# Norm rows in the activation buffer, weight-sum work in eighths, score requests per channel tile

## The chip, the cores and the metric

The kernel runs on one core of one Trainium2 chip. The time is device microseconds of that core for one execution; the comparison number is the median of several. TensorE (PE) multiplies matrices, PEld is its loading of weights, VectorE (DVE) works element by element, ScalarE (ACT) applies functions and copies, GpSimd (POOL) is used only to build constants, SyncE (SP) issues nearly all DMAs. Every engine executes its own instructions in program order and waits on semaphores for the others.

## The reference

Two layers, each a sliding attention block A and a gated feed-forward block B, with residuals; the weights are the same in both layers. x is 2048 tokens by 1024 in bf16.

```python
def _A_ref(x, wqkv, wo):          # 32 heads of 32
    W, dil = 8, 2
    ...                           # q, k, v = x @ wqkv
    idx = pos[:, None] - off[None, :]      # off = 0, 2, ..., 14
    logits = jnp.einsum("bhsd,bhswd->bhsw", q, kg) * scale
    attn = _softmax(logits, axis=-1)       # masked before the start
    o = jnp.einsum("bhsw,bhswd->bhsd", attn, vg)
    return o... @ wo
def _B_ref(x, w1, w3, w2):        # 1024 -> 3584 -> 1024
    return (silu(x @ w1) * (x @ w3)) @ w2
x = A_x
x = x + _A_ref(_layernorm(x, axis=-1), A_wqkv, A_wo)
x = x + _B_ref(_layernorm(x, axis=-1), B_w1, B_w3, B_w2)
x = x + _A_ref(_layernorm(x, axis=-1), A_wqkv, A_wo)
x = x + _B_ref(_layernorm(x, axis=-1), B_w1, B_w3, B_w2)
```

A token attends to itself and to seven earlier ones at steps of two.

## The kernel before, in words

**Units and order.** Tokens are cut into four chunks of 512; a unit is a layer and a chunk, so there are eight units, (layer 0, chunks 0 to 3) and (layer 1, chunks 0 to 3). First comes QKV of layer 0 for all chunks (`first_q` for q of chunk 0, then `q_part` for the rest, L682). Then, for each unit u, `b_stage` (L854) does its feed-forward; in units 1 to 4 it is followed by layer 1's QKV of unit u+3. Attention is worked in halves of 256 tokens, 16 in all, on VectorE, beside the matrix work of TensorE.

**The planner.** The order on each engine is written out by the program itself. It keeps an estimated clock per engine (`now`, moved by `pe`, `dve` and `act` with fixed costs) and queues of small steps for VectorE: norms, sums, value steps, score steps, in this priority. `background(until)` (L130) emits from the queues whatever fits before a given estimated time. The order is therefore fixed when the program is built; an engine that is late in reality still waits in that order.

**Norms.** `norm_stats` (L203) and `norm_apply` (L223) normalise a 128-token tile: statistics L210, L213, L215, then L234 writes the normalised rows `xn` (128 by 1024, fp16) to one of three buffers of the pool `xnp`, and L237 issues a DMA transpose on SP that puts them into `xnT`, the operand of the next matmuls. A buffer is free again when its transpose has landed. The key of a norm is ("Q", layer, chunk) for QKV and ("B", layer, chunk) for the feed-forward. `hT` (L171), 128 by 16 by 512 bf16, holds the feed-forward activations (L895, L792; read at L908); `first_q` keeps q of chunk 0 in its first eight slices (L339, stored by L386).

**Attention on VectorE.** For a half, `score_steps` (L460) multiplies q by shifted k eight times (L475) and folds them in a tree into `psm` (L399, L401); then a gather on TensorE (L488) sums over the head's channels into `L`; softmax L507 to L519 (the exponential on ScalarE, L511); then four spreads on TensorE (L528), each copied by ScalarE into `At` (L530). `value_steps` (L540) multiplies At by shifted v (L559) and folds into `oT`. `o_tile` (L630) multiplies oT by wo (L646) and adds it to x (L651); after a half's second tile the feed-forward norm is queued. The score steps of the next half start when the four spreads are out.

**Requests to TensorE.** A gather or a spread is put into `pe_queue` with its estimated time. `pe_requests(limit=1)` (L454) puts up to `limit` of them into TensorE's order, those whose time plus 1.5 us has come by TensorE's estimated clock. It is called by `between` (L665), which also loads due weights and places output tiles: in QKV after two channel tiles (16 matmuls), in `b_stage` of units 0 and 1 before every block of 128 features, in the w2 products after each accumulator, in `products` (L760, units 2 to 7) after each product. `between(..., must=True)` places all queued output tiles, and forces the value and score steps they need inline; in a unit it stands at L923, at the second accumulator of the last w2 stage's first half, where `hold` is not set.

**Feed-forward.** Units 0 and 1 (u < TU) do it directly. A group is four blocks of 128 features; per block (`fi`) come eight matmuls with w1 (L883), silu to `sg` on ScalarE (L887), eight matmuls with w3 (L891), and L895 on VectorE, hT = sg * up. Groups 0 to 3 are the first split, 4 to 6 the second; each split ends with the w2 products (L908). Units 2 to 7 use a seven-product scheme (`products`) on sums of weight blocks, which units 0 (w1) and 1 (w3) make on the way, in `prepare` (L748):

- `measure` (L715): ScalarE takes the sum of absolute values of the group's weight tile; its output goes to a scratch that covers the first 4096 columns of `big`;
- `scales` (L721): a small matmul (L724) sums over partitions, four small VectorE operations make a power-of-two scale and its inverse;
- `transform(a)` (L734), a = 0, 1: four scaled copies on ScalarE (L739) into block a of `big`, four differences on VectorE (L744), and a DMA to DRAM (`t_d`, L746). Block 0 lies inside the scratch of `measure`, block 1 does not.

One of these four steps stands at the end of each block of the group:

```python
        if fi == 0:
            measure(u, g, w)
        elif fi == 1:
            scales(u, g)
        elif fi == 2:
            transform(u, g, w, 0)
        else:
            transform(u, g, w, 1)
```

Weights come in tiles of 1 MB through six buffers (`wp`), loaded in the order `seq`; a group's two tiles are given back by `release(2)` and reloaded at the next `between`.

Of the kernel before, what the change touches and what calls it, by code (L numbers as in the profile page):

```python
# [17 lines left out]
def kernel(  # L18
# [129 lines left out]
    def bank(name):  # L148
        return psum.tile([P, 512], FP32, name=name, tag="mm")
# [73 lines left out]
    def norm_apply(key, c, r):  # L223

        if key not in xnTs:
            xnTs[key] = xtp.tile([P, KT, CH], FP16, name="xnT")
        xnT = xnTs[key]
        mv, sd, ready = moments[key, r]
        rstd = small.tile([P, 2], FP32, name="rstd")

        def apply(i):
            j = 2 * r + i
            xn = xnp.tile([P, D], FP16, name="xn")
            nc.vector.tensor_scalar(xn[:], x_sb[:, c * TPC + j, :], mv[:, i, 0:1], rstd[:, i:i + 1],  # L234
                                    op0=ALU.subtract, op1=ALU.mult)
            with hp():
                nc.sync.dma_start_transpose(out=xnT[:, :, j * P:(j + 1) * P], in_=xn[:])  # L237
            xnT_at[key] = now["dve"] + DMA
            norm_left[key] = norm_left.get(key, TPC) - 1

        yield 0.10, ready, lambda: nc.vector.reciprocal(rstd[:], sd[:])
        for i in range(2):
            yield 0.47, 0.0, lambda: apply(i)
# [421 lines left out]
    def between(hold, must=False):  # L665

        flush()
        pe_requests()
        while o_queue and (must or oT_at.get((o_queue[0][0], o_queue[0][1] // 2), 1e9) + 0.3 <= now["pe"]):
            o_tile()  # L670
            if not must:
                break
        while norm_queue and not hold:
            queue_norm(*norm_queue.pop(0))
            if not norm_queue and sum_queue:
                adds.append([sum_later(sum_queue.pop(0)), None])
# [5 lines left out]
    def q_part(l, c, which, ws, then=()):  # L682

        ready = ready_norm(("Q", l, c))
        xnT = xnTs[("Q", l, c)]
        first = (l, c, which) == (0, 0, 1)
        if first:
            qT = qkvp.tile([P, KT, TCH], BF16, name="qT")
            kT = qkvp.tile([P, KT, HALO + TCH], BF16, name="kT")
            nc.vector.memset(kT[:, :, 0:HALO], 0.0)  # L690
        for t0 in range(0, KT, SG):
            sgt = stg.tile([P, SG, CH], BF16, name="sgt")
            for t in range(t0, t0 + SG):
                ps = bank("ps")
                for kk in range(KT):
                    nc.tensor.matmul(ps[:], lhsT=ws[kk // KH][:, kk % KH, t::KT], rhs=xnT[:, kk, :],  # L696
                                     start=(kk == 0), stop=(kk == KT - 1))
                r = pe(KT, ready)
                background(r)
                nc.scalar.copy(sgt[:, t - t0, :], ps[:])  # L700
                done = act(0.6, r)
                if first:
                    nc.scalar.copy(kT[:, t, HALO:], ps[:, 0:TCH])
                    done = act(0.4)
            nc.sync.dma_start(qkv_d[l][which][:, t0:t0 + SG, c * CH:(c + 1) * CH], sgt[:])
            if first and t0 == SG:
                load_part(qT, 0, 0, 0, False)
            between(False)
            if t0 // SG < len(then) and then[t0 // SG]:
                then[t0 // SG]()  # L710
        qkv_at[l, c, which] = done + DMA / 2
        if first:
            qks[0, 0] = qT, kT, done + 0.1
# [17 lines left out]
        nc.vector.reciprocal(down, up)  # L731
        dve(0.8, r)

    def transform(m, g, w, a):  # L734

        b = blocks[a]
        KQ = KT // 2
        for i, (kh, fh) in ((0, (0, 0)), (1, (0, 1)), (3, (1, 0)), (5, (1, 1))):
            nc.scalar.activation(b[:, i], w[:, kh * KQ:(kh + 1) * KQ, fh * 256 + a * P:fh * 256 + (a + 1) * P],  # L739
                                 ACTF.Copy, scale=up_scale[:, m, g:g + 1])  # L740
        r = act(2.9, now["dve"] + 0.1)
        background(r)
        for out, x, y in ((4, 5, 1), (1, 1, 0), (2, 5, 1), (6, 3, 2)):
            nc.vector.tensor_tensor(b[:, out], b[:, x], b[:, y], op=ALU.subtract)  # L744
        dve(1.4, r)
        nc.sync.dma_start(t_d[m][g][:, a, :], b.rearrange("p b k c -> p (b k c)"))  # L746

    def prepare(u, g, fi, w1t, w3t):  # L748

        w = (w1t, w3t)[u]  # L750
        if fi == 0:
            measure(u, g, w)
        elif fi == 1:
            scales(u, g)
        elif fi == 2:
            transform(u, g, w, 0)
        else:
            transform(u, g, w, 1)

    def products(u, f0, f1, hold):  # L760

# [92 lines left out]
    def b_stage(u, hold):  # L854
# [7 lines left out]
        for (f0, f1) in fsplits:  # L862
            lastsplit = (f1 == fsplits[-1][1])
            if u >= TU:
                th = products(u, f0, f1, hold)
                if lastsplit:
                    sums_free[0] = True
            for g0 in range(f0, f1, FG) if u < TU else ():
                gn = min(FG, f1 - g0)
                w1t, w3t = weight("w1"), weight("w3")  # L870
                for fi in range(gn):
                    f = g0 + fi
                    slack = 1.0 if f < f1 - 2 else -0.5
                    if f < f1 - 1:
                        between(hold)
                    else:
                        flush()
                    if f == 8 and 1 <= u and u + 3 < len(units):
                        lq, cq = units[u + 3]
                        queue_norm(("Q", lq, cq), cq, range(R))  # L880
                    pg = bank("pg")
                    for kk in range(KT):
                        nc.tensor.matmul(pg[:], lhsT=w1t[:, kk, fi * P:(fi + 1) * P], rhs=xnT[:, kk, :],  # L883
                                         start=(kk == 0), stop=(kk == KT - 1))
                    r = pe(KT, ready)
                    sg = sgp.tile([P, CH], BF16, name="sg")
                    nc.scalar.activation(sg[:], pg[:], ACTF.Silu)  # L887
                    ts = act(0.6, r, "silu")
                    pu = bank("pu")
                    for kk in range(KT):  # L890
                        nc.tensor.matmul(pu[:], lhsT=w3t[:, kk, fi * P:(fi + 1) * P], rhs=xnT[:, kk, :],  # L891
                                         start=(kk == 0), stop=(kk == KT - 1))
                    r = max(pe(KT), ts)
                    background(r + slack)
                    nc.vector.tensor_tensor(hT[:, f - f0, :], sg[:], pu[:], op=ALU.mult)  # L895
                    th = dve(0.64, r)
                    prepare(u, g0 // FG, fi, w1t, w3t)
                release(2)
            for hh in range(2):
                w2ts = [weight("w2") for g0 in range(f0, f1, 8)]  # L900
                for j in range(TPC):
                    n = c * TPC + j
                    final = u == len(units) - 1 and lastsplit and hh == 1 and j == TPC - 1
                    step = 256 if final else 512
                    for q0 in range(0, 512, step):
                        acc = psum.tile([P, step], FP32, name="acc", tag="mm")
                        for f in range(f0, f1):
                            nc.tensor.matmul(acc[:], lhsT=hT[:, f - f0, j * P:(j + 1) * P],  # L908
                                             rhs=w2ts[(f - f0) // 8][:, (f - f0) % 8, q0:q0 + step],
                                             start=(f == f0), stop=(f == f1 - 1))  # L910
                        if q0 == 0:
                            pe(f1 - f0 - 1)
                            r = pe(1, th)
                            background(r + 1.0)
                            dve(0.64, r)
                        o0 = hh * 512 + q0
                        xs = x_sb[:, n, o0:o0 + step]
                        nc.vector.tensor_tensor(xs, xs, acc[:], op=ALU.add)  # L918
                        if last and lastsplit:
                            nc.sync.dma_start(xout[:, n, o0:o0 + step], xs)  # L920
                    if j == TPC - 1:
                        release(2)
                    between(hold and not lastsplit, lastsplit and hh == 0 and j == 1 and not hold)  # L923
# [78 lines left out]
```

## Time and profile before

| what | value |
|---|---|
| median of 8 runs | 1670.11 us (1665.77 to 1673.2) |
| profiled execution | 1669.68 us |
| its span | 1668.0 us |
| granted TensorE clock, mean | 0.987 |
| DMA queue 1 | 376.22 MB, 70.2% of 16 engines |
| HBM | 216 GB/s over the span |

The span runs from the first to the last instruction; the execution's time is 1.7 us more. Busy times are of one profiled execution. Where TensorE's matmuls follow each other without a wait, 16 of 512 columns take 3.45 us. "[7.23 <-DVE vT L428]" behind an instruction says that its engine was idle for 7.23 us before it, until VectorE's instruction of line 428 released it. A line that a profile names is the line of the kernel printed above.

### The profile page before, as it was taken

How to read it: one execution, taken by the hardware profiler on the slowest of the kernel's cores; microseconds unless marked ns; L12 is line 12 of the kernel's file. 1: busy time of each engine (PE TensorE's matmuls, PEld its weight loads, DVE VectorE, ACT ScalarE, POOL GpSimd, SP SyncE). 2: the span in 40 equal slices, each digit the busy share in tenths (PEclk: the TensorE clock that was granted, in tenths of full speed). 3: DMA queues.
4: the chain of work that ended last, by engine and by line, in shares of the span. 5: the costliest groups of instructions: out<-in, count | busy, mean ns of one | idle time of the engine just before them, and what ended most of it. 6: DMA issues, size and time to landing. Idle time of an engine off the chain costs nothing.

```text
span 1668.0 us, 24367 instructions
## 1 busy us (share of the span) xinstructions
PE 1586.4 (95%) x9779; PEld 1014.4 (61%) x9844; DVE 1223.6 (73%) x2180; ACT 643.8 (39%) x1001; POOL 3.4 (0%) x16
## 2 busy tenths in 40 slices
PE   9899999978999999999999999999999999998999
PEld 7465544433444468485685757756586758585866
DVE  4764868869687778987487875879669798985423
ACT  3333275352826336051451414422253416161422
POOL 0000000000000000000000000000000000000000
PEclk9999999998999999999999999999999999999999
DMA  9444676764875868686696777958687769585954
GB/s 306 136 136 126 196 227 214 224 215 131 258 231 194 267 212 297 197 275 202 238 284 220 251 201 266 294 199 261 200 279 249 239 220 326 188 272 176 323 183 148
DMA packets 298785, 377.90 MB, mean 227 GB/s; under 512 B 71472, under 2 KB 234672, under 8 KB 298544
## 3 DMA queue, kind: packets, MB, share of 16 engines
q1 hardware_dynamic: 298528, 376.22, 70.2%
q8 instruction: 77, 1.26, 0.3%
q14 instruction: 36, 0.29, 0.0%
q10 hardware_dynamic: 144, 0.13, 0.0%
HBM read 305.53 MB, written 55.05 MB: 216 GB/s over the span
## 4 chain that ended last, share of the span: by engine, by line
PE 63%; DVE 22%; DMA 7%; ACT 6%; issue 2%; SPq 0%; ACTq 0%; DVEq 0%
PE st L778 22%; PE acc L908 22%; PE ps L696 8%; PE po L646 6%; DVE pr L475 3%; DMA xnT<-xn 3%; DVE tm L559 3%; DVE pr L399 3%; DVE tm L399 3%; ACT big L718 2%; DVE st L210 2%; DMA t_d<-big 2%; PE pg L883 1%; DVE hT L792 1%; ACT big L739 1%
## 5 line engine op out<-in xcount | busy, mean ns | idle before, releaser
L908 PE MATMUL acc<-w2t,hT 128*128 128x512 bf16 (+1 forms) x1765 | 391.0, 378 | 2.1
L696 PE MATMUL ps<-xnT,wqkv 128*128 128x512 f16 (+1 forms) x1469 | 327.5, 383 | 0.2
L908 PEld LDWEIGHTS <-hT 128*128 128x128 bf16 x1804 | 176.4, 98 | 208.5 <-issue 0.5
L778 PEld LDWEIGHTS <-early 128*128 128x128 f16 x2688 | 262.7, 98 | 43.4 <-issue 8.3
L696 PEld LDWEIGHTS <-wqkv 128*128 128x128 bf16 x1472 | 211.2, 144 | 112.5 <-issue 7.6
L778 PEld LDWEIGHTS <-late 128*128 128x128 f16 x2016 | 197.0, 98 | 36.5 <-issue 12.1
L559 DVE TENSOR_TENSOR tm<-At,vT 128x2048 bf16<-128x2048 bf16 x128 | 156.1, 1220 | 65.8 <-ACT At L530 65.7
L700 ACT CAST sgt<-ps 128x512 bf16<-128x512 f32 x184 | 104.0, 589 | 230.5 <-PE ps L696 123.8
L778 PE MATMUL st<-big,early 128*128 128x256 f16 x1344 | 172.7, 273 | 5.9 <-ACT st L804 5.6
L778 PE MATMUL st<-xnT,late 128*128 128x256 f16 x1344 | 174.1, 273 | 2.7 <-DVE big L826 2.1
L778 PE MATMUL st<-xnT,early 128*128 128x256 f16 x1344 | 163.6, 273 | 0.1
L475 DVE TENSOR_TENSOR pr<-qT,kT 128x2048 bf16<-128x2048 bf16 x128 | 156.1, 1220 | 0.0
L646 PE MATMUL po<-wo,oT 128*128 128x512 bf16 x494 | 120.6, 389 | 21.5 <-DVE oT L401 20.4
L399 DVE TENSOR_TENSOR tm<-tm 128x1024 bf16<-128x1024 bf16 (+1 forms) x256 | 137.8, 553 | 0.4
L399 DVE TENSOR_TENSOR pr<-pr 128x1024 bf16<-128x1024 bf16 (+1 forms) x256 | 137.6, 555 | 0.5
L918 DVE TENSOR_TENSOR x_sb<-x_sb,acc 128x512 bf16<-128x512 bf16 x129 | 87.3, 678 | 67.3 <-PE acc L908 66.4
L804 ACT COPY st<-st 128x512 f32<-128x512 f32 x84 | 48.4, 577 | 183.6 <-PE st L778 142.0
L883 PE MATMUL pg<-xnT,w1t 128*128 128x512 f16 x448 | 109.0, 387 | 0.2
L891 PE MATMUL pu<-xnT,w3t 128*128 128x512 f16 x448 | 106.6, 381 | 0.0
L646 PEld LDWEIGHTS <-oT 128*128 128x128 bf16 x512 | 50.5, 99 | 85.4 <-DVE oT L401 26.8
L787 ACT ACTIVATE sg<-st,down_scale 128x512 bf16<-128x512 f32 x126 | 87.0, 691 | 37.9 <-PE st L778 36.9
L792 DVE SCALAR_TENSOR_TENSOR hT<-st,down_scale,sg 128x512 bf16<-128x512 f32 x126 | 93.1, 746 | 8.9 <-PE st L778 8.0
(119 smaller groups left out, 1271.9 us busy)
## 6 DMA issues: line engine op xcount, KB each, us to landing
early<-t_d SPq DMA_DIRECT2D x84, 1024.0 KB, 7.2
late<-t_d SPq DMA_DIRECT2D x84, 768.0 KB, 6.6
w2t<-in_B_w_dram SPq DMA_DIRECT2D x48, 1024.0 KB, 7.8
wqkv<-in_A_wqkv_dram SPq DMA_DIRECT2D x28, 1024.0 KB, 7.7
t_d<-big SPq DMA_DIRECT2D x28, 896.0 KB, 4.5
qkv_d<-sgt SPq DMA_DIRECT2D x92, 256.0 KB, 2.4
w1t<-in_B_w_dram SPq DMA_DIRECT2D x14, 1024.0 KB, 7.0
w3t<-in_B_w_dram SPq DMA_DIRECT2D x14, 1024.0 KB, 9.4
```

Of the source, the lines that this page charges most:

```text
L399: nc.vector.tensor_tensor(b[:, 0:m, :], b[:, 0:m, :], b[:, m:2 * m, :], op=ALU.add)
L475: V.tensor_tensor(pr[:], qT[:], kT[:, :, k0:k0 + TCH], op=ALU.mult)
L559: V.tensor_tensor(tm[:], At[:], win, op=ALU.mult)
L646: nc.tensor.matmul(ps[:], lhsT=oT[:, t, j * P:(j + 1) * P], rhs=wo[:, t, hh * 512:(hh + 1) * 512], start=(t == 0), stop=(t == KT - 1))
L696: nc.tensor.matmul(ps[:], lhsT=ws[kk // KH][:, kk % KH, t::KT], rhs=xnT[:, kk, :], start=(kk == 0), stop=(kk == KT - 1))
L700: nc.scalar.copy(sgt[:, t - t0, :], ps[:])
L778: nc.tensor.matmul(out[:, a, :], lhsT=w[:, a, blk, k, :], rhs=rhs[:, k, :], start=start and a == 0 and k == 0, stop=k == KQ - 1, skip_grou ...
L792: nc.vector.scalar_tensor_tensor(hT[:, f:f + 2, t0:t0 + HT], src, inv, gates[g, q][:], op0=ALU.mult, op1=ALU.mult)
L883: nc.tensor.matmul(pg[:], lhsT=w1t[:, kk, fi * P:(fi + 1) * P], rhs=xnT[:, kk, :], start=(kk == 0), stop=(kk == KT - 1))
L891: nc.tensor.matmul(pu[:], lhsT=w3t[:, kk, fi * P:(fi + 1) * P], rhs=xnT[:, kk, :], start=(kk == 0), stop=(kk == KT - 1))
L908: nc.tensor.matmul(acc[:], lhsT=hT[:, f - f0, j * P:(j + 1) * P], rhs=w2ts[(f - f0) // 8][:, (f - f0) % 8, q0:q0 + step], start=(f == f0), ...
L918: nc.vector.tensor_tensor(xs, xs, acc[:], op=ALU.add)
```

## The change

There are three edits.

1. In `norm_apply`, for keys ("Q", layer 0), that is the norms of chunks 1, 2 and 3 before layer 0's QKV, the normalised rows are not written to a pool buffer. Each of a chunk's four tiles has its own place in `hT`, two of its slices from slice 8 on, read as fp16. The transpose reads from there.
2. `between` asks for up to two requests instead of one, and `q_part` also asks (up to two) after the first channel tile of each pair.
3. `prepare` is called twice per block, between the w1 and the w3 matmuls and after L895, with a slot from 0 to 7. `transform` is split into `copies` and `differences`. Measuring is in slot 2, scales and the copies of block 0 in slot 5, the copies of block 1 in slot 6, the differences of block 0 in slot 7; the differences of block 1 are in slot 1 of the next group (for the last group in its slot 7). Each `differences` issues its store.

```diff
@@ norm_apply
-            xn = xnp.tile([P, D], FP16, name="xn")
-            nc.vector.tensor_scalar(xn[:], x_sb[:, c * TPC + j, :], mv[:, i, 0:1], rstd[:, i:i + 1],
+            if key[0] == "Q" and key[1] == 0:
+                xn = hT[:, KT + 2 * j:KT + 2 * j + 2, :].rearrange("p a t -> p (a t)").bitcast(FP16)
+            else:
+                xn = xnp.tile([P, D], FP16, name="xn")[:]
+            nc.vector.tensor_scalar(xn, x_sb[:, c * TPC + j, :], mv[:, i, 0:1], rstd[:, i:i + 1],
...
-                nc.sync.dma_start_transpose(out=xnT[:, :, j * P:(j + 1) * P], in_=xn[:])
+                nc.sync.dma_start_transpose(out=xnT[:, :, j * P:(j + 1) * P], in_=xn)
@@ between
-        pe_requests()
+        pe_requests(2)
@@ q_part, after the copy of a channel tile
+                if t < t0 + SG - 1:
+                    pe_requests(2)
@@ transform
-    def transform(m, g, w, a):
+    def copies(m, g, w, a):
...
-        r = act(2.9, now["dve"] + 0.1)
+        act(2.9, now["dve"] + 0.1)
+
+    def differences(m, g, a):
+
+        b = blocks[a]
+        r = now["act"] - 2.9 * (1 - a)
         background(r)
...
@@ prepare
-    def prepare(u, g, fi, w1t, w3t):
+    def prepare(u, g, slot, w1t, w3t):
 
         w = (w1t, w3t)[u]
-        if fi == 0:
+        if slot == 1 and g:
+            differences(u, g - 1, 1)
+        elif slot == 2:
             measure(u, g, w)
-        elif fi == 1:
+        elif slot == 5:
             scales(u, g)
-        elif fi == 2:
-            transform(u, g, w, 0)
-        else:
-            transform(u, g, w, 1)
+            copies(u, g, w, 0)
+        elif slot == 6:
+            copies(u, g, w, 1)
+        elif slot == 7:
+            differences(u, g, 0)
+            if g == NG - 1:
+                differences(u, g, 1)
@@ b_stage
                     ts = act(0.6, r, "silu")
+                    prepare(u, g0 // FG, 2 * fi, w1t, w3t)
...
-                    prepare(u, g0 // FG, fi, w1t, w3t)
+                    prepare(u, g0 // FG, 2 * fi + 1, w1t, w3t)
```

## The prediction

> **What bounds the kernel now.** I read first the busy times of the page, then what TensorE waited for, then those places in the timeline, then the chain that ended last.
>
> ```profile
> PE 1586.4 (95%) x9779; PEld 1014.4 (61%) x9844; DVE 1223.6 (73%) x2180; ACT 643.8 (39%) x1001; POOL 3.4 (0%) x16
> ```
>
> TensorE is the bound: 95% busy, and its stream is one fixed order. What can be won is its waits and the slow clock after them. The waits of PE, by line and releaser (total us, times, longest):
>
> ```profile
> PE po L646 <- DVE oT L401: 20.4, 11, 4.9
> PE size L724 <- ACT big L718: 16.7, 10, 3.5
> PE L L488 <- DVE psm L401: 9.3, 4, 3.5
> PE L L488 <- DVE vT L428: 7.2, 1, 7.2
> ...
> PE pe L528 <- DVE An L519: 3.3, 1, 3.3
> ```
>
> The rest of that list is 14.8 us at L778, in the feed-forward of units 2 and later, which the diff does not touch, and 2.5 us of small waits, nearly all in the first 11 us. I place the rows above by stage; the first feed-forward matmul starts at 212.19, layer 1's first QKV at 572.88.
>
> **Layer-0 QKV.** The timeline shows who is late there (start, length, [idle before <-releaser]):
>
> ```profile
> 39.33 0.55 DVE L234 TENSOR_SCALAR xn<-x_sb,mv,rstd 128x1024 f16<-128x1024 bf16 x1 [10.17 <-DMA xnT<-xn]
> ...
> 69.62 0.62 PE L488 MATMUL L<-psm,gather 128*32 128x512 bf16 x4 [7.23 <-DVE vT L428]
> 70.17 12.49 PE L696 MATMUL ps<-xnT,wqkv 128*128 128x512 f16 x48
> ...
> 83.01 0.55 DVE L234 TENSOR_SCALAR xn<-x_sb,mv,rstd 128x1024 f16<-128x1024 bf16 x1 [9.11 <-DMA xnT<-xn]
> ```
>
> In each of the chunks 1, 2 and 3 the fourth tile's norm waits for one of the three xn buffers, that is for a transpose to land (10.17, 9.11 and 8.09 us; 39.0 us with four later ones in layer 1). VectorE is in order, so the score products behind it are late, and TensorE waits at the gather (L488, 7.23 and 3.48 us) and the spread (L528, 3.27), then at L646 (0.85 + 0.27): 15.1 us. After a wait the matmuls also run slowly: the 48 of 70.17 take 12.49 us; at the usual 0.2158 us (16 in 3.45) 10.4, and 0.1 of start, so 2.0 lost; after 145.69, 32 take 8.53 instead of 6.9, 1.6 lost. Together **18.7 us**.
>
> **Feed-forward of units 0 and 1.** The L724 waits are all here: 1.94, 1.06, 2.73, 0.32, 1.62, 0.95, 1.67, 3.54, 1.19, 1.68. The chain that ended last shows why (start, us, what):
>
> ```profile
> 238.25 2.55 ACT big L739 x4
> 242.69 4.96 DMA t_d<-big
> 247.75 3.72 ACT big L718 x2
> 252.13 1.73 PE pg L883 x8
> ```
>
> Copies, differences, the store of the weight sums, then the next group's measuring, whose scratch overlaps block 0, then TensorE. After 268.68 eight matmuls take 3.21 us instead of 1.73, after 461.32 sixteen take 3.44 + 2.44 instead of 3.46: 3.9 more. **20.6 us.** The other loss is the forced output projection at 363 to 381:
>
> ```profile
> 359.80 0.38 PE L528 MATMUL pe<-An,spread 128*128 128x512 bf16 x1
> ...
> 367.92 0.61 PE L646 MATMUL po<-wo,oT 128*128 128x512 bf16 x1 [4.94 <-DVE oT L401]
> ```
>
> Its half's first spread ran at 344.39, the last at 362.60 (one per check), so the 17.5 us of value products stand bare in front of TensorE: waits 14.94 us, and 1.4 for 25 matmuls in 6.79 instead of 5.4: **16.3 us**. The same happens once more at 1505 to 1508: 1.88 + 2.49, and 20 matmuls in 5.74 instead of 4.3: **5.8 us**.
>
> **The change, part by part.**
>
> *Rows in hT.* The 12 L234 of layer 0 keep their 0.55 us and 12 transposes (1.28 us of SP each); only the buffer wait goes. The four places of a chunk are separate, and were last read a chunk earlier. Without the wait the fourth tile starts at 29.16, statistics (8 tiles by 1.40 = 11.2) end at 40.9, the score tree of 18.5 us (50.99 to 69.5 now) at 59.4. TensorE reaches the gather at 62.4 in today's order, at 60.7 if it is asked for one channel tile earlier. What is late next: the load of qT, behind the four transposes on SP (issued at 41.82, would be some 5.5 us earlier, at 36.3; with the 4.3 us of such loads it lands at 40.6, just in time). The spread and the second gather follow the same way: their DVE chains lose 9.1 and 8.1 us against waits of 3.27 and 3.48. I take 17 of 18.7; if qT's load takes the place of the first wait, 9.5; at best 18.7.
>
> *Score requests.* The spreads of a half go two per check, and in QKV the check comes after each channel tile (1.73 us) instead of each second one. At 85.93 to 96.94 four spreads took 11 us while VectorE idled 12.46; now about 2. Together with the waits above each half of layer 0 starts its value tree earlier: the second half gains some 10 + 18 us, the later ones what they then find free. VectorE is only 125 of the first 200 us busy, so the work exists to be pulled forward. At 344.39 the two-per-check rule alone would finish the spreads at 347.9, 15 us before the forced projection; with 28 us more in hand the value tree is over by then. I take the whole 16.3; if only the spreads help, about 60% of 12 us of VectorE is free, and 7 remains won. The second forced place: three idle stretches of 15.46, 18.05 and 19.72 us of VectorE before L559 in layer 1's QKV shrink by about 9 each, more than the 4.37 it lacks. I take 5.8, at worst 0. Against it: a gather asked for up to a channel tile earlier finds VectorE less ready. In layer 1's QKV it waits today 1.58, 0.78 and 3.49; four such stages by half a tile (0.86) is 3 us lost; ends 12 lost (four by 3) and 6 won (those waits gone). Queued behind a waiting gather are all later matmuls, so such a wait counts whole.
>
> *Weight sums.* Nothing is removed: measuring (3.72), copies (2 by 2.55), differences (2 by 1.8), four scale operations and two stores per group stay. Measuring starts after the second gate, not the first, and the size matmul comes three matmul groups later (5.2 us) instead of two and a bit. But the loop through block 0 stays: measuring 3.8, sg 0.6, hT 0.65, scales 0.6, copies 2.55, sg 0.6, hT 0.65, differences 1.8, store to measuring 3.7 to 5.1 (346.08 and 247.75): 15.0 to 16.4 us, against 14.0 us of TensorE per group (8 by 1.73, and the size matmul). A first group has 0.85 us in hand, so second groups wait about 0.8 (four of them), later ones about 1.7 (six): 13.4. Output tiles of 3.45 us, which now come up inside groups since the halves are earlier, lengthen some four groups and take about 1.2 each: 9 left. Waits below 3 us mostly leave the clock alone, so I take 20.6 - 9 = 11.6. Ends: 20.6 (every loop covered), and -3 (ten waits of 2.4). The store of block 1 moves behind the next group's weight loads on SP, and hides there: weights are loaded two groups (27 us) ahead and land in 7.0 and 9.4 us.
>
> Sum: 17 + 16.3 + 5.8 - 3 + 11.6 = 47.7 us. The profiled execution took 1669.68 (span 1668.0; median of the eight 1670.11, 0.4 above): **1622 us**.
>
> Two rules, beside the sum. The trace pays for a slow clock after 2.73 us at 268.68, and not after 3.27 at 85.93 (16 matmuls in 3.45 directly behind). The Trainium skill ("TensorE: Matmul & The Clock Gate", Part 1) halves the rate after an idle window of about 3.4 us that runs free of the program; taken as a threshold it would make the weight-sum term's clock loss 2.4 instead of 3.9, and the sum 46. And the trace switches ScalarE's table in 1.28 us, with the next activation 0.02 later. The skill ("ScalarE: Activation LUTs", What ACT_TABLE_LOAD costs) says 2.66 with its drain, which speaks against packing more between the gates: by it each softmax would add 2.8 us to a loop, by four halves some 11, and the sum would be 37; the trace decides against it.
>
> **Rivals.** *The loop decides*: measuring only changes its phase, and the waits of 20.6 stay. For it: the loop above is longer than a group. Against it: output tiles inside groups. Time 1622 + 11.6 = 1634, to 1647 with the lower end of one other part. *All is covered*: 18.7 + 20.6 + 16.3 + 5.8 + 6 = 67.4, 1602. *The rows don't do it*: qT's load, or the place in hT, holds the norm as the buffer did: 17 lost, and some of the lead with it, 1639 to 1660. For it: a transpose issued at 30.09 took 9.21 us to land under the weight loads. *Slower*: requests come before VectorE is ready. The six gathers in QKV stages could each wait 3.49 (the longest without the buffer wait), their spreads 3.27, and 2.0 of clock: 8.8 by six is 53, 1675. It decides from 8 us per such half; against it, the spreads have 3.9 us in hand at 154.60 and 6 at 344.39.
>
> **Numbers.** Forecast (1612 to 1632) 45%; the loop (to 1647) 25%; all covered (1602 to 1612) 15%; rows don't do it 8%; slower 5%; within 0.2%, about what a measurement of this kernel can tell from no change, 2%. The range 1603 to 1647 leaves out the last three and the edges. Faster 0.93, same 0.02, slower 0.05.
>
> **What would show it.** Right: no L234 wait before 212; no PE wait at L488 or L528 in layer-0 QKV, first feed-forward matmul at about 194; L724 waits of about 9 us in total; no L646 waits. Wrong: L724 waits above 15; new L488 waits of 3 us and slow clock behind them; VectorE without idle time in units 0 and 1, which would make it the bound.

## The result and the profile after

| (matmuls: us from the start of the span) | before | after |
|---|---|---|
| median of the runs | 1669.94 us (1663.73 to 1679.48, 32 runs) | **1657.23 us** (1656.15 to 1660.84, 11 runs) |
| span of the profiled execution | 1668.0 us | 1654.7 us |
| first feed-forward matmul | 212.19 | 204.23 |
| first feed-forward matmul of unit 1 | 404.40 | 385.15 |
| first QKV matmul of layer 1 | 572.88 | 563.18 |

The ratio is 0.9927, 95% interval [0.9914, 0.994]: 12.2 us of 1670 faster. Forecast were 1622 us, a gain of 47.7; the time lies outside the range of 1603 to 1647. Below, a gain or loss "by the ratio" is the distance of the ratio from 1, times 1670. The new code moves the lines: L724 (size) is now L729, L718 (measure) L723, L739 (copies) L744, the differences L744 are L754, the gather L488 is L491, the output projection L646 L649, pg L883 and pu L891 are L898 and L907.

First the account of TensorE. Its busy time, which contains the slow clock, from part 1 of the page:

```profile
PE 1592.0 (96%) x9777; PEld 1018.3 (62%) x9844; DVE 1222.9 (74%) x2180; ACT 643.7 (39%) x1000; POOL 3.4 (0%) x16
```

and its waits by line and releaser (total us, times, longest):

```profile
PE size L729 <- ACT big L723: 26.2, 8, 5.2
...
PE L L491 <- DVE psm L404: 6.7, 3, 3.8
PE L L491 <- DVE vT L431: 4.6, 1, 4.6
```

All waits together went from 74.2 to 55.5 us, busy time from 1586.4 to 1592.0: -18.7 and +5.6 make -13.1, and the spans differ by 13.3. The account closes on TensorE, so no other bound has to be looked for. Inside it, the output projection doesn't wait any more (20.4 before), the gathers wait 11.3 in place of 16.5, and **the size matmul waits 26.2 in place of 16.7**, in fewer and longer waits. What such a wait costs besides its own length is read from TensorE's timeline:

```profile
432.57 0.58 PE L729 MATMUL size<-size,ones 128*128 128x1 f32 x2 [3.32 <-ACT big L723]
433.02 3.57 PE L898 MATMUL pg<-xnT,w1t 128*128 128x512 f16 x8
436.38 2.90 PE L907 MATMUL pu<-xnT,w3t 128*128 128x512 f16 x8
439.12 1.89 PE L898 MATMUL pg<-xnT,w1t 128*128 128x512 f16 x8
```

The sixteen matmuls between 433.02 and 439.12 take 6.10 us in place of 3.45: 2.65 us more, behind a wait of 3.32.

Why the wait is there is seen in the chain that ended last, just ahead of it (start, us, what):

```profile
414.29 0.04 DVE tm L562
...
415.43 0.68 DVE hT L911
...
417.36 1.14 DVE tm L562
...
421.30 0.60 DVE hT L911
421.90 0.35 DVE big L754
...
423.68 4.97 DMA t_d<-big
...
428.81 3.71 ACT big L723 x2
```

The size matmul before ran at 413.35, the copies of block 0 from 416.66 to 419.22. The differences (L754) could follow, but VectorE is in order, and value products (tm, L562), their folds and an hT stand in front. They begin at 421.82, 2.60 us behind the copies; before the change, at 433.57, they began right behind them. The scales too stand behind an hT (415.43) that stands behind a value product. The loop from size matmul to size matmul was 19.2 us here; over the eight pairs of neighbouring groups without output tiles between them it was 17.4 to 19.3 us, against 14.0 of TensorE's own work. Output tiles stand inside two pairs alone (from 242.54 and from 347.03); behind those the size matmul waits for nothing.

In layer-0 QKV the timeline answers to the one of before at 69.62:

```profile
30.06 10.52 SPq L240 DMA_TRANSPOSE xnT<-hT  x4
41.26 0.62 SPq L434 DMA_DIRECT2D qT<-qkv_d  x1
46.46 1.22 DVE L478 TENSOR_TENSOR pr<-qT,kT 128x2048 bf16<-128x2048 bf16 x1 [5.44 <-DMA qT<-qkv_d]
65.14 0.62 PE L491 MATMUL L<-psm,gather 128*32 128x512 bf16 x4 [4.56 <-DVE vT L431]
```

No norm waits for a row buffer before 212, as forecast. But the four transposes hold SP for 10.52 us all the same (11.04 before), qT's load is issued at 41.26 and not at 36.3, and the first gather still waits 4.56.

### The profile page after: what moved, and what is told of

Read it like the earlier page. It is cut to its first block, busy times and chain, and to the rows that moved or that the text cites. A ratio compares the mean times of both kernels' runs of the same rounds, so it can differ in the third digit from the quotient of the medians.

```text
span 1654.7 us, 24338 instructions
## 1 busy us (share of the span) xinstructions
PE 1592.0 (96%) x9777; PEld 1018.3 (62%) x9844; DVE 1222.9 (74%) x2180; ACT 643.7 (39%) x1000; POOL 3.4 (0%) x16
## 4 chain that ended last, share of the span: by engine, by line
PE 73%; DVE 15%; DMA 6%; ACT 4%; issue 1%; SPq 1%; ACTq 0%; DVEq 0%
PE st L793 25%; PE acc L924 22%; PE ps L699 13%; PE po L649 7%; PE pg L898 3%; PE pu L907 2%; DVE st L210 2%; DMA xnT<-xn 2%; DVE pr L478 2%; ACT big L723 2%; DVE tm L562 2%; DMA qkv_d<-sgt 2%; DVE pr L402 2%; DMA t_d<-big 1%; DVE tm L402 1%
## 5 line engine op out<-in xcount | busy, mean ns | idle before, releaser
L924 PE MATMUL acc<-w2t,hT 128*128 128x512 bf16 x1764 | 389.5, 378 | 2.0
L562 DVE TENSOR_TENSOR tm<-At,vT 128x2048 bf16<-128x2048 bf16 x128 | 156.2, 1220 | 66.7 <-ACT At L533 66.6
L898 PE MATMUL pg<-xnT,w1t 128*128 128x512 f16 x448 | 115.5, 405 | 2.1 <-ACT sgt L703 2.1
L649 PE MATMUL po<-wo,oT 128*128 128x512 bf16 x490 | 113.6, 379 | 1.2
L907 PE MATMUL pu<-xnT,w3t 128*128 128x512 f16 x448 | 109.7, 389 | 0.0
L831 DVE TENSOR_TENSOR st<-st,big 128x512 f32<-128x512 f32 x84 | 58.5, 696 | 51.8 <-ACT big L828 51.5
```

Of the source, the lines that this page charges most:

```text
L562: V.tensor_tensor(tm[:], At[:], win, op=ALU.mult)
L649: nc.tensor.matmul(ps[:], lhsT=oT[:, t, j * P:(j + 1) * P], rhs=wo[:, t, hh * 512:(hh + 1) * 512], start=(t == 0), stop=(t == KT - 1))
```

## The experiments

The theory after this result: the rows gain most of what was forecast, the requests take away the forced projection, and the eighths lose, because the loop through block 0 got longer. The rivals: the rows or the requests do not do what they were to do, or the requests fill VectorE in units 0 and 1 and it is they that make the loop longer. The runs show some of both for the loop.

### The parts alone

**Rows alone**: the kernel before with the first hunk of the diff (`norm_apply`).

> The kernel before with the first edit alone (layer-0 QKV norms written into hT). My theory (the eighths lengthen the loop through block 0, the rest of the change gains): the first gather still waits about 4.6 us behind qT's load, the size waits stay near 17 us, the forced projection at 363 to 381 stays; 6 to 10 us faster than before, ratio about 0.995. Rival (the rows do nothing by themselves, since SP is held by the transposes all the same): within 2 us of before.

1658.18 us, ratio 0.9907 [0.9881, 0.9932], a gain of 15.5 us by the ratio (11.4 to 19.9). The first feed-forward matmul came at 198.16, 14.0 earlier. TensorE's waits:

```profile
PE po L649 <- DVE oT L404: 20.4, 11, 4.9
PE size L727 <- ACT big L721: 16.8, 10, 3.5
```

The forced projection and the size waits are as before. The gain is above the 6 to 10 us expected, and the first gather waits 3.05, less than the 4.6.

**Eighths alone**: the kernel before with the hunks of `transform`, `prepare` and `b_stage`.

> The kernel before with the weight-sum edit alone. My theory: the loop measuring, scales, copies, differences, store, measuring becomes longer, since block 0's differences now stand behind the next block's product on VectorE; size waits 22 to 28 us with a slow clock behind them; 6 to 14 us slower than before, ratio 1.004 to 1.008. Rival (the waits of 26 us come from the value products that the earlier spreads put between on VectorE, not from the eighths): size waits at or below 16.7 us and no slower than before, ratio 0.995 to 1.000.

1681.89 us, ratio 1.0056 [1.0037, 1.0076]: 9.4 us **slower** (6.2 to 12.7), where the prediction had a gain of 11.6. The line that carries it, to be held against 16.7, 10, 3.5 before:

```profile
PE size L724 <- ACT big L718: 22.7, 10, 3.7
```

The loss sits in the loop. There are ten intervals from one group's size matmul to that of the next group in the same split. In the kernel before they are 14.87 to 18.41 us, 162.36 in all; here 15.93 to 18.95, 174.54 in all. The 12.2 us more are the whole difference of the two spans (1668.0 and 1680.2). On average the copies begin 1.9 us behind the size matmul (3.5 before), the differences 2.2 behind the end of the copies (0.4 before), and the next measuring 7.0 behind the start of the differences (6.0 before): block 0's store lands 4.6 to 5.6 us after its issue, where eight of the ten took 3.6 to 3.8 before. In four of the ten, background work stands between copies and differences; in the other six it is hT alone, as here:

```profile
343.32 0.59 PE L724 MATMUL size<-size,ones 128*128 128x1 f32 x2 [3.09 <-ACT big L718]
343.77 3.57 PE L893 MATMUL pg<-xnT,w1t 128*128 128x512 f16 x8
...
345.02 2.56 ACT L739 ACTIVATE big<-w1t,up_scale 128x512 f16<-128x512 bf16 x4 [1.27 <-DVE up_scale L730]
347.14 2.85 PE L902 MATMUL pu<-xnT,w3t 128*128 128x512 f16 x8
...
350.10 0.69 DVE L906 TENSOR_TENSOR hT<-sg,pu 128x512 bf16<-128x512 bf16 x1 [4.97 <-PE pu L902]
...
350.70 1.80 DVE L749 TENSOR_TENSOR big<-big 128x512 f16<-128x512 f16 x4
```

The hT ahead of the differences waits for a product (pu) that runs slowly because of the size wait just before it. So here a wait lengthens the next loop. The rival, that the eighths alone cost nothing, fell.

**Requests alone**: the kernel before with the hunks of `between` and `q_part`.

> The kernel before with both request edits alone. My theory: the forced projection's wait (14.9 us, and 4.4 at 1505) goes, the buffer waits of layer-0 QKV stay; size waits near 17; 12 to 18 us faster, ratio about 0.991. Rival: size waits rise towards 26 since VectorE is fuller there; then 3 to 8 us faster.

1665.56 us, ratio 0.9954 [0.9935, 0.9973], a gain of 7.7 us (4.5 to 10.9), where 19.1 were forecast.

```profile
PE size L726 <- ACT big L720: 25.1, 8, 4.7
PE L L488 <- DVE psm L401: 16.0, 4, 5.5
PE L L488 <- DVE vT L428: 8.8, 1, 8.8
```

The rival's numbers came (3 to 8 us, size waits towards 26). No row of the output projection is left: both forced places are gone. But the size waits grew by 8.4 and the gather waits from 16.5 to 24.8. The timeline of this kernel in unit 1 shows what stands between copies and differences:

```profile
439.06 2.54 ACT L741 ACTIVATE big<-w3t,up_scale 128x512 f16<-128x512 bf16 x4
...
442.62 0.55 DVE L234 TENSOR_SCALAR xn<-x_sb,mv,rstd 128x1024 f16<-128x1024 bf16 x1 [2.08 <-DMA xnT<-xn]
443.09 1.22 DVE L559 TENSOR_TENSOR tm<-At,vT 128x2048 bf16<-128x2048 bf16 x1
444.22 0.28 DVE L401 TENSOR_TENSOR oT<-tm 128x256 bf16<-128x256 bf16 x1
444.43 1.79 DVE L746 TENSOR_TENSOR big<-big 128x512 f16<-128x512 f16 x4
```

The copies end at 441.60; a norm that waits for its buffer and a value product, both let in earlier by the planner, come first.

**Rows and requests**: the change without its weight-sum edit.

> The change without its weight-sum edit. My theory: faster than the whole change by what the eighths cost, some 12 to 16 us: about 1643, ratio to before 0.984; size waits 14 to 18. Rival (the size waits come with the earlier value products): size waits 24 or more, and the time is that of the change or longer, 1657 to 1665.

1650.99 us, ratio 0.9873 [0.9852, 0.9894], a gain of 21.2. The parts add up: 15.5 + 7.7 = 23.2 against 21.2 measured together, and with the eighths 15.5 + 7.7 - 9.4 = 13.8 against the change's 12.2. So the change is slower with its third edit than without it, by 6.2 us in the medians and 9.0 by the ratios. The expectation and its rival both missed: the time lies between theirs, and the size waits (23.2) just below the rival's 24. And the size waits are high with the requests wherever the rows are: 25.1 and 23.2 us with them, 16.7 and 16.8 without. The fuller VectorE of the rival is in this line; that it acts through what stands ahead of the differences is seen at the place shown above, and only argued for the others.

### The request after each channel tile

**Rows and two requests per check**, with the check after each pair of channel tiles as before, and without the eighths.

```diff
-        pe_requests()
+        pe_requests(2)
```

> The rows in hT and two requests per check, without the check after each channel tile and without the weight-sum edit. Theory (the check per channel tile asks for gathers and spreads before VectorE is ready, and so takes back part of what the pairs win): the first feed-forward matmul at 199 to 201 instead of 206, gather waits at most 8 us in all instead of 16.3; about 1644, 6 to 7 us faster than with the per-tile check (1651). Rival (the pairs themselves do the harm, by filling VectorE in units 0 and 1): 1650 or slower, with size waits of 23 us and more unchanged.

1646.2 us (1637.77 to 1651.84), ratio 0.9839 [0.9799, 0.9879]. The gathers wait 9.1 us in place of the 16.3 of rows and requests with the check after each tile, and the first feed-forward matmul comes at 198.0 in place of 205.95:

```profile
PE size L727 <- ACT big L721: 22.9, 9, 4.9
...
PE L L491 <- DVE psm L404: 5.0, 2, 2.8
PE L L491 <- DVE vT L431: 3.5, 1, 3.5
```

The gain over that kernel, 4.8 us in the medians, lies within overlapping intervals, and the profiled execution was the fastest of the four, 8.4 us under their median. The gather waits point the same way, but the gain is not shown. The forced projection is gone here too, so beside the rows `limit=2` is enough to take it away; the size waits are as high as there.

### The loop through block 0

**Own scratch, quarters**: as the last kernel, but measuring writes to buffers of the staging pool in four pieces, so it need not wait for the store of block 0. The four sums per group cost one more reduction on VectorE.

```diff
-        junk = big[:, 0:4096].bitcast(BF16)...
-        nc.scalar.activation(junk, w[:], ACTF.Abs, accum_out=size[:, m, g:g + 1])
+        for i in range(4):
+            junk = stg.tile([P, SG, CH], BF16, name="sgt")
+            nc.scalar.activation(junk[:], w[:, 2 * i:2 * i + 2, :], ACTF.Abs, accum_out=size[:, m, g, i:i + 1])
```

> As the run before it, and measuring writes into the staging buffers of QKV (in four pieces of 1024 columns, their four sums added by one more VectorE operation) and no longer over block 0; quarters, not eighths. Theory (the loop through block 0's store is what TensorE waits for at the size matmul): size waits from above 20 us to below 6, the slow clock in units 0 and 1 gone with them, 18 to 26 us faster than with the shared scratch: about 1622. Rival (ScalarE or VectorE are simply too full in these units): size waits stay above 12 us and the gain is below 10.

1631.67 us, ratio 0.9755 [0.9735, 0.9776]: 14.5 us better in the medians, less than the 18 to 26 expected. Neither expectation fits: the size waits stay at 17.0, where the theory had less than 6, and the gain is above the rival's 10. No measuring waits for block 0's store any more. One piece of the first measuring waits 2.74 us (at 205.32) for the QKV store of the staging buffer it takes over; ahead of all others ScalarE is not idle, so what makes them late is what stands before them on ScalarE.

**Own scratch, the whole change**: the same edit on the changed kernel.

> The whole change, with the same scratch in the staging buffers. Theory (loop through block 0): size waits from 26 us to below 5, 25 to 32 us faster than the change: about 1629. Rival (VectorE's value products between the steps): size waits above 12, gain below 12.

**1624.51 us** (1621.54 to 1626.44), ratio 0.9707 [0.9683, 0.9732], the best kernel of this study: 32.7 us under the change in the medians.

```profile
PE size L730 <- ACT sgt L724: 9.2, 4, 4.7
```

Size waits below 5 were expected; here too ScalarE is not idle ahead of any measuring, so what is left is not the store. Of the 30.0 us between the two spans (1654.7 and 1624.7) 17.0 are size waits; TensorE's busy time, with the slow clock in it, falls from 1592.0 to 1582.8; the other waits keep their sum (29.3 and 29.0). So most of the missing time hangs on the shared buffer. That 1624.5 stands next to the 1622 forecast for the change, and 9.2 next to its 9 us of size waits, confirms nothing: the forecast's 9 came from the loop through block 0, which this kernel doesn't have.

**Differences at once**: the whole change with its shared scratch, but the differences of block 0 stand directly behind its copies (slot 5), and the planner lets no background work in between.

> The whole change, with block 0's differences directly behind its copies (slot 5) and no background work ahead of them, so that its store leaves earlier. Theory (the loop through block 0's store, lengthened by VectorE's wait for the next product and by background work): the loop becomes 3 to 4 us shorter, size waits from 26 to 8 to 14 us, 10 to 16 us faster than the change: about 1645. Rival (the store's landing time of 5 us under the weight loads is what lengthens it): waits above 20, gain below 6.

1644.15 us, ratio 0.9828 [0.9806, 0.985], 13.1 better than the change in the medians. The timeline shows the short loop, from the copies of one group to the measuring of the next:

```profile
393.11 2.56 ACT L744 ACTIVATE big<-w3t,up_scale 128x512 f16<-128x512 bf16 x4 [1.93 <-DVE up_scale L735]
395.70 1.80 DVE L755 TENSOR_TENSOR big<-big 128x512 f16<-128x512 f16 x4 [2.48 <-ACT big L744]
...
402.69 3.62 ACT L723 ACTIVATE big<-w3t 128x4096 bf16<-128x4096 bf16 x1 [1.65 <-DMA t_d<-big]
```

Differences 0.03 us behind the copies, and a size matmul at 391.48 and 406.45: 15.0 us. Five of the ten pairs of neighbouring groups are at 15.0 to 15.1, the lower end of the loop that the prediction had worked out (15.0 to 16.4). The size waits fall to 12.9; 17.3 of gather waits and 5.1 of output projection come instead; that the background work, held back here, is what makes these late is argued, not shown. The scratch is the better way out.

**Own scratch, eighths, check after each pair.** The whole change with its own scratch, without the hunk of `q_part`.

> The change with the request after each channel tile taken out again, and with a measuring scratch of its own, so that measuring no longer waits for the store of block 0. Theory (the check after each tile only made gathers come too early: 16.3 against 9.1 us of gather waits without it; the eighths are good once the shared scratch is gone): 5 to 7 us less than the 1624.5 of the change with its own scratch, 1618 to 1620, gather waits of 6 to 9 us, no waits of the w2 products for hT. Rival 1 (the check after each tile brings as much in early value products as it costs in gather waits): 1624, within 2. Rival 2 (eighths cost time in themselves, not through the scratch): 1632 or more, the time of quarters with their own scratch.

1631.13 us, ratio 0.9761 [0.9736, 0.9785]: the theory fell. The time is the second rival's, the time of quarters with their own scratch, but not for its reason, that eighths cost time in themselves. Against quarters with the same check (0.9755 [0.9735, 0.9776]) the eighths are worth nothing that can be told. And with eighths and own scratch the check after each tile is worth 6.6 us in the medians (0.9707 [0.9683, 0.9732] against 0.9761), not a loss. A line of this kernel's timeline shows one cost:

```profile
348.52 7.34 PE L649 MATMUL po<-wo,oT 128*128 128x512 bf16 x25 [4.28 <-DVE oT L404]
```

One forced projection is back: 4.28, and 25 matmuls in 7.34 in place of 5.4, 6.2 us together. Quarters with own scratch and the check after each tile would complete the square. That kernel deadlocks, its engines waiting for one another, and has no time, so what of the 6.6 needs the eighths stays open.

### Why the first gather still waits

**Rows, and qT and kT of layer 0 loaded from GpSimd's queue**, past the transposes on SP.

```diff
-            nc.sync.dma_start(tl[:], qkv_d[l][which]...
+            queue.dma_start(tl[:], qkv_d[l][which]...      (GpSimd if l == 0 and which < 2)
```

> The kernel before with the first edit only (rows in hT), and the loads of qT and kT in layer 0 issued by GpSimd in place of SP. Theory (the load of qT for the first half stands behind four transposes that hold SP for 10.5 us, and that is why the first gather still waits 5): qT is issued by 37, the score products start by 42.5 in place of about 46.5, the first gather waits under 2 us in place of 5.3, the 48 matmuls behind it run at full rate, and the first feed-forward matmul comes 4 to 7 us earlier than 198.16, about 193; the time falls by 3 to 7 from 1658.2, to 1651 to 1655. Rival (the DMA engines are full there, or q itself is stored late, so that qT lands no earlier whoever issues it): the score products start at 46 as before, and the time stays at 1658, within 2.

1655.35 us, ratio 0.9908 [0.9886, 0.9931], as without it. The timeline:

```profile
30.05 12.34 SPq L240 DMA_TRANSPOSE xnT<-hT  x4
30.14 1.02 POOL L435 DMA_DIRECT2D qT<-qkv_d  x1 [26.05 <-DMA qkv_d<-hT]
...
44.97 0.58 ACT L704 CAST sgt<-ps 128x512 bf16<-128x512 f32 x1 [9.16 <-DMA qkv_d<-sgt]
...
46.81 1.23 DVE L479 TENSOR_TENSOR pr<-qT,kT 128x2048 bf16<-128x2048 bf16 x1 [6.39 <-ACT kT L707]
```

qT was issued at 30.14 and landed 8.6 later, yet the score products began at 46.81 as before. They now wait for kT, which ScalarE copies; ScalarE stood 9.16 us in front of a staging buffer whose store waits behind the transposes.

**The stores of q and k of chunk 0 from GpSimd too.**

> The kernel before with the first edit, with the loads of qT and kT of layer 0 issued by GpSimd, and the stores of q and k of chunk 0 too. Theory (with the loads alone moved, qT landed at 38.8, but ScalarE stood 9.16 us in front of a staging buffer whose store waits behind the transposes on SP, so that kT was complete only at 46.8; both the load and the stores are held by SP): ScalarE no longer stands there, the score products start at 41 to 42, behind the last statistics, the first gather of layer 0 waits less than 0.5 us, and the first feed-forward matmul comes at 194 to 196 in place of 198.16; the time is 1650 to 1655 (1658.2 with the first edit alone). Rival (the DMA engines, at a share of 1.0 to 1.2 there, hold the stores themselves): the score products start at 44 or later, and the wait at the gather stays at 2 to 5 us.

1664.28 us, ratio 0.9956 [0.993, 0.9981]: no gain, rather a loss against rows alone. The rival's late score products came, and more:

```profile
27.48 22.56 SPq L240 DMA_TRANSPOSE xnT<-hT  x4
...
49.02 0.59 ACT L704 CAST sgt<-ps 128x512 bf16<-128x512 f32 x1 [16.84 <-DMA qkv_d<-sgt]
...
52.56 1.23 DVE L479 TENSOR_TENSOR pr<-qT,kT 128x2048 bf16<-128x2048 bf16 x1 [12.35 <-ACT kT L707]
```

The four transposes now hold SP for 22.56 us, and the store that ScalarE waits for lands at 49.0, when they are nearly through (50.04). The first gather waits only 1.53, below the rival's 2 to 5, because TensorE has already waited 5.43 for a copy of kT. So taking the stores off SP's queue does not free them: the transfers themselves are late.

**The same loads with own scratch and eighths**: the kernel of 1631.13 us with qT and kT from GpSimd.

> The kernel of the first of these three runs, with the qT and kT loads of layer 0 issued by GpSimd in place of SP. Theory: the same 3 to 7 us off, 1612 to 1616; rival (transfer bound there): no difference from that run, within 2 us.

1638.11 us, ratio 0.9804 [0.9781, 0.9827]: 7.0 us worse in the medians. Neither theory nor rival; nothing is gained by the other queue.

## Why the prediction was wrong, step by step

**What bounds the kernel**: right. TensorE's waits and slow clock hold the whole difference.

**Rows**: forecast 17, measured 15.5 alone (11.4 to 19.9). The L234 waits before 212 went, as said. Wrong was a step inside: qT's load "at 36.3". It assumed that SP was held by the missing row; the transposes hold it for 10.5 us with no buffer to wait for, and the first gather keeps 3.05 (rows alone) to 4.56 us (the change). For a late qT the prediction had a gain of 9.5, and 15.5 came all the same, so the near hit of the term is in part luck.

**Score requests**: forecast 16.3 + 5.8 - 3, 19.1; measured 7.7 (4.5 to 10.9). The mechanism was right: all 20.4 us of output projection waits went, at both forced places and the 1.1 us in layer-0 QKV. The step that failed is that the work pulled forward costs nothing ("the work exists to be pulled forward"): it stands between the steps of the weight-sum loop (size waits 16.7 to 25.1), and the earlier gathers waited 8.3 more where 3 were put. The waits in the later units at L778, which the prediction had put aside as untouched, fell as well, from 14.8 to 7.5 us: the cost is larger than the 11.4 us that are missing.

**Weight sums**: this term decided, and its sign was wrong. Forecast +11.6 (20.6 to -3), measured -9.4 alone, beyond the lower end. The step: "the loop through block 0 stays ... 15.0 to 16.4 us". With the eighths alone it is 15.9 to 19.0, in the change 17.4 to 19.3. At 413.35 to 432.57 of the change its pieces are: size matmul to copies 3.31 (forecast 1.85), copies 2.56, copies to differences 2.60 (1.25), differences to measuring 6.99 (5.5 to 6.9), measuring to size 3.76. What lies above the forecast is here mostly VectorE's value products ahead of scales and differences; ScalarE's two copies of At (413.20, 1.05) ahead of the first sg add to it. With the eighths alone, background work stands ahead of the differences in four of the ten loops, hT is late behind sg or a slow product in three more, and the store lies at the long end of its 3.7 to 5.1 us or above in nearly all. I summed the loop as if only its own sg and hT stood in it; the planner fills VectorE between. That the loop would be the same length whatever its slots was the mistake, and the kernel with the differences at once has 15.0 in half of its pairs.

**The sum**: 35.5 us are missing. Weight sums account for 21.0 of them (11.6 + 9.4), requests for 11.4, rows for 1.5; 1.6 is left, well inside the intervals.

**Rivals**: "the loop decides" named the right mechanism, but took the waits of before as its worst case, 1634 to 1647. "The rows don't do it" (1639 to 1660) holds the time, but not for its reason. The sign that was given, "L724 waits above 15", was the one that came. The two rules beside the sum would have moved it to 46 and 37; neither is what was missing.

## What to carry to other kernels

A buffer that two engines and a store share makes a loop, and the loop's length is set by everything that stands in front of each of its steps on in-order engines, background work included: sum it from the queue, not from its own steps. Work that is pulled forward is not free when it lands between the steps of such a loop; take the shared buffer away first (here 14.5 us with quarters, 32.7 with the change), and then judge the other edits again, for here the check after each tile and the eighths changed their worth with it.

## What the runs showed of the hardware

**A second queue made the transfers slower.** With stores and loads on GpSimd beside four transposes on SP, the windows view gives from 32 to 40 us (length; PE, PEld, DVE, ACT and POOL busy; then PEclk, DMA share, GB/s):

```profile
32.00:36.00 4.00, 3.95 (x19) 2.66 (x19) 3.90 (x10) 0.18 (x1) 0.32 (x1) 1.00 1.24 165
36.00:40.00 4.00, 4.00 (x20) 2.64 (x19) 3.90 (x9) 0.00 (x0) 0.00 (x0) 1.00 1.36 50
```

and with the rows alone, everything on SP:

```profile
36.00:40.00 4.00, 4.00 (x20) 2.65 (x19) 3.93 (x9) 0.00 (x0) 0.00 (x0) 1.00 1.21 209
```

The packets begun in the 4 us from 36 took 1.36 of the sixteen engines' time for 50 GB/s (a packet counts whole where it begins), against 1.21 for 209. The Trainium skill ("DMA: Bandwidth & Descriptors", Rules for kernel authors) says that spreading DMAs over the issuing engines doesn't help bandwidth, since all run on the same 16 engines. The runs agree (1655.35 with the loads on GpSimd against 1658.18 us), and go further: transposes of 10.44 us took 22.56. The page of that run lists GpSimd's transfers as a queue of another kind (q0, software_dynamic); whether a second queue of SP's kind would do the same was not measured.

**The clock after short waits.** In the change, eight matmuls behind a wait of 1.93 us at 451.57 took 3.36 us; in the whole change with its own scratch, eight behind a wait of 1.93 at 408.82 took 1.89. So the length of a wait does not fix its price, and the prediction's "waits below 3 us mostly leave the clock alone" was too kind. The clock records show what it goes by. They change only in steps of 3.41 us: the slow stretches of the kernel before last 3.41, 6.83 or 17.07, but for the one that ends the span. Cut at these steps, the change:

```profile
448.67:452.08 3.41, 1.48 (x9) 0.63 (x8) 1.02 (x4) 3.33 (x3) 0.00 (x0) 1.00 1.06 353
452.08:455.50 3.42, 3.42 (x10) 1.21 (x9) 3.32 (x9) 2.23 (x4) 0.00 (x0) 0.50 1.23 341
```

and the whole change with its own scratch:

```profile
404.39:407.80 3.41, 2.50 (x12) 0.95 (x10) 3.31 (x8) 3.41 (x8) 0.00 (x0) 1.00 0.96 246
407.80:411.22 3.42, 2.40 (x12) 1.22 (x13) 3.35 (x8) 3.03 (x5) 0.00 (x0) 1.00 1.07 358
411.22:414.63 3.41, 3.41 (x17) 1.57 (x16) 3.20 (x12) 2.55 (x4) 0.00 (x0) 1.00 1.06 388
```

In the first the wait lies whole in one step (TensorE busy 1.48 of 3.41), and the next step runs at 0.50; in the second it is cut into 0.91 and 1.02, and the clock stays at 1.00. Over the fourteen traces, from 20 us on, no full-speed step with less than 1.6 us of idle TensorE was followed by a slow one (6353 steps), 11 of 53 with 1.6 to 2.0 us were, and 95 of 96 with more. The prediction's odd wait fits as well: the 3.27 us before 85.93 were cut into 1.7 and 1.6.
